# Handing the issue order of three engines to the scheduler, up to the last round of a Fourier transform and mixture-of-experts kernel

## Chip, core and metric

One core of one Trainium2 chip. The metric is the device time of one execution in microseconds (us); lower is better. TensorE (PE in the profile; PEld is its weight load), VectorE (DVE), ScalarE (ACT), GpSimd (POOL) and SyncE (SP, which only starts transfers here) each run their own instructions in the order in which the program lists them for that engine, and wait for one another through semaphores.

## The reference

The input `x` is 8 batches of 2496 tokens of 256 numbers. First a two-dimensional Fourier transform of each batch, of which the real part is kept; then every token goes to one of 8 experts:

```python
X = fft(fft(x, axis=1), axis=2).real          # per batch
x = X.reshape(19968, 256)
e_idx = argmax(x @ w_gate, axis=1)
gate_w = softmax(x @ w_gate)[e_idx]; eom = sigmoid(x @ w_output_gate)
for e in range(8):                             # F = 1024
    h = relu(x[e_idx == e] @ w1[e]); ye = h @ w2[e]
    out[e_idx == e] = gate_w * eom[:, e] * ye
```

## The kernel before, in words

There are two bodies of work. The **background** makes tokens, the **foreground** uses them.

*Background*, per batch b of 8, in five chunks: `xt` comes in by SP (512 KB each); `fold1` and `fold2` (L387 to L430) fold it by symmetry, on VectorE for batches under PF = 3, with `fold1` on GpSimd for the others; `square` (L383) or the activation in `fold2` sums its energy for a scale; `dstage` (L451) is the transform along the features, fp32 matmuls into PSUM; `devac` (L467) splits the result into two fp16 halves `ahi` and `alo` (ScalarE writes the first, VectorE the second); `sstage` (L513) is the transform along the sequence, fp16 matmuls; `sevac` (L528) combines its results into `rows`; `gating` (L564) chooses the expert and the destination row in some 30 small VectorE instructions with a matmul pair (L603, L604) among them; `scatter` (L667) writes 128 rows at a time to the DRAM buffer `scr`, sorted by expert, on GpSimd's queue. After certain batches `table_a` (L748) fixes which 256-row blocks are full; `table_b` (L766) does so for what is left.

*Foreground*: `experts` (L1363) goes through slots of up to 256 rows of one expert. The slots are grouped into rounds (ROUNDS, L40): three slots after batch 0, 13 after batch 1, 16 after batch 3, 16 after batch 5, and then the last round of 27 pairs and some smaller blocks after batch 7. For a slot, `load_x_` (L1213) brings the rows by a transposing transfer `xr` on SP; `load_w` (L1229) brings fp32 weights into `raw`; `conv` (L1258) splits them into two fp16 halves, ScalarE first (L1264) and VectorE after it (L1265), 1024 columns at a time, into a single weight buffer `wbuf`; `wenergy` (L1243) sums their squares on ScalarE. `mm1` (L1272) does 12 matmuls into the PSUM tile `hp` for each of four groups g of a slot; ScalarE (L1288, `hh`) and then VectorE (L1289, `hl`) take it out. `mm2` (L1291) does 12 matmuls into `yp`; after the fourth group ScalarE (L1311, `y`) takes it out and GpSimd's queue sends it to `out` (L1312). `hp` has two PSUM buffers and `yp` has one until the last round, `psb_t` (background) has two, `psm_t` one.

*Order.* The text writes an order by hand. In `experts` the `mm2` of a group comes LAG = 3 groups behind its `mm1`; `conv` calls stand between the groups. `start` (L926) writes the first batch, much of the second and the first weights line by line, and mixes three threads by weights (L1059). `background` (L1432) is a generator; the main loop (L1507 to L1523) takes a piece of it after each foreground step, paced by WORK (L66) and by cost figures that the pieces yield. `gating` and the folds yield pauses (GAP, L63), in which the other pieces go ahead.

`tc.manual_schedule()` makes every engine issue its instructions in the order of the text. With a set of engines, only those keep the order of the text; for the others the compiler's scheduler picks, each time an engine is free in its own simulated run of the program, among the instructions whose inputs it takes as ready, the one that stands first in the text. The order that it finds is fixed in the program; nothing is reordered on the chip. The data dependencies and the buffers are the same either way. Before the change one such region, with every engine, holds all of it:

```python
    with tc.manual_schedule():
        fg = experts()
        start(lambda: next(fg))
        rp.close()
        ...
        for m in fg:          # slots, with background() between them, until table_b is done
            ...
        for m in fg:          # the rest of the slots
            pass
```

Of the kernel before, what the change touches and what calls it, by code (L numbers as in the profile page):

```python
# [63 lines left out]
LB = 5  # L64
PF = 3
WORK = ((28.0, 13), (94.0, 112), (86.0, 140), (62.0, 117))  # L66
CONV = [mybir.EngineType.Activation, mybir.EngineType.DVE]
BIG = float(1 << 20)

# [158 lines left out]
def fft_moe_kernel(ctx: ExitStack, tc: tile.TileContext, xl, wg, w1, w2, tde, tdo, gt, ts0, tsm, tsr, tsq, cst, tid, out):  # L228
# [48 lines left out]
    if True:  # L277
# [17 lines left out]
        def load_x(n=NB * KC):  # L295

            while n and len(xq) < NB * KC:
                q = pw if held[pw] < NX2 and len(xq) < 2 * KC else px
                if held[q] == (NX2 if q is pw else NX):
                    break  # L300
                held[q] += 1
                b, c = divmod(len(xq), KC)
                t = q.tile([128, 8, HN], F32, name="xt", tag="xt", bufs=NX2 if q is pw else NX)
                nc.sync.dma_start(t, xl[b, c])
                xts[b, c] = t
                xq.append(q)
                n -= 1
# [205 lines left out]
        def sstage(b, i):  # L513
            s = st[b]
            if i == 0 and not routed(b):
                s["rows"] = []
                s["qs"] = pg.tile([128, 10, 32], F32, name="qs", tag="qs")
            ps = s["sps", i] = pool["b"].tile([128, 2, 512], F32, name="psb_t", tag="b")
            for k in range(2):
                for trig in range(2):  # L520
                    w = 129 if routed(b) else 145
                    src = 161 if routed(b) and trig else 145 * trig
                    for lhs, rhs, kw in s_terms(s, i, k, trig):
                        nc.tensor.matmul(ps[:, k, w * trig:w * trig + w], lhs, rhs[:, src:src + w], **kw)  # L524
                if k == 0:
                    yield "s"
# [617 lines left out]
    if True:  # L1144
# [8 lines left out]
        def add_wbuf(p_):  # L1153
            i = len(wbuf)
            wbuf.append([[p_.tile([128, 2, 1024], F16, name=f"w{m}b{i}{h}", bufs=1) for h in range(2)] for m in range(2)])
# [93 lines left out]
        def changed(n):  # L1249

            if n not in fresh:
                t, w, qi = table(n)
                need(sched[n][0])
                fresh.clear()
                fresh[n] = nc.values_load(t[0:1, 2 * w + qi:2 * w + qi + 1], engines=CONV, min_val=0, max_val=1)
            return fresh[n]
# [175 lines left out]
    def background():  # L1432
        def rest():
            yield from evac(1, 0)
            yield from c_s(1, 2)
            for _ in table_a(1):
                yield 0.13, 0
            scq.append(lambda: ready.add(1))

        yield from mix((g_(1), 2.0), (rest(), 12.0), (f_(2), 5.0))  # L1440
        yield from mix((c_d(2), 1.0))
        for b in range(2, NB):
            ths = [(c_s(b), 16.0)]
            if b + 1 < NB:
                ths.append((f_(b + 1), 11.0))
            yield from mix(*ths)
            for k, a in enumerate(BAS):
                if b == a and k not in begun:
                    scq.append(lambda k=k: k in begun or early(k, nc.sync.dma_start(fence, scr[DUM:DUM + 1, 0:1])))
            ths = [(g_(b), 9.5)]  # L1450
            if b + 1 < NB:
                ths.append((c_d(b + 1), 5.0))
            yield from mix(*ths)
            if b + 1 in BAS:
                k = BAS.index(b + 1)
                for _ in table_a(k):
                    yield 0.13
                scq.append(lambda k=k: ready.add(k))
        while scq:
            scq.pop(0)()  # L1460
        xp.close()
        for fill in (lambda: None, pads):
            fill()
            while deferred:
                deferred.pop(0)()
                yield 0.4
        for _ in table_b():
            yield 0.15
        pps.close()
        lp.close()  # L1470
        fx.append(pl(ctx, name="fr2", bufs=2))
        psf["h"] = pl(ctx, name="fpe2", bufs=1, space=PS)
        psf.update(hb=3, yb=2)
        add_raw(fx[1])
        add_wbuf(fx[1])
        ready.add(LAST)
# [7 lines left out]

    add_raw(fr0)
    add_wbuf(fr0)
    with tc.manual_schedule():
        fg = experts()
        start(lambda: next(fg))
        rp.close()  # L1490
        fx.append(pl(ctx, name="fr", bufs=2, side="right"))
        pps.close()
        pps = ExitStack()
        psf["h"] = pl(ctx, name="fpe", bufs=1, space=PS)
        psf.update(hb=2, yb=1)
        pool["b"] = pl(pps, name="psb2", bufs=2, space=PS)
        pool["m"] = pl(pps, name="psm2", bufs=1, space=PS)
        sums["t"] = pool["m"].tile([128, 512], F32, name="psm_t", tag="m")

        for i in range(2):  # L1500
            for _ in sstage(1, i):
                pass
        next(fg)
        load_x()
        bg = background()
        seg, acc, slot = 0, 0.0, 0
        for m in fg:  # L1507
            tick[0] += 1
            if m[0] == "slot":
                slot = m[1] + 1  # L1510
            while slot >= FIRST[seg + 1] - 1 and seg + 1 < LAST:
                seg += 1
            if scq and (tick[0] % 2 or not seg):
                scq.pop(0)()
            work, quanta = WORK[seg]
            acc = min(acc + work / quanta, 2.5)
            while acc > 0:
                c = next(bg, None)
                if c is None:
                    break  # L1520
                acc -= c
            if LAST in ready:
                break  # L1523
        for m in fg:
            pass

# [27 lines left out]
```

## Time and profile before

| | us |
|---|---|
| median of 2 runs | 1258.42 (1257.29 to 1259.56) |
| profiled execution, its own time | 1257.77 |
| its span, first to last instruction | 1256.0 |
| PE busy in the span | 1096.6 (87%) |
| DVE, ACT, POOL busy | 691.6, 608.5, 411.6 |
| mean granted TensorE clock | 0.941 of full |

The span is what the profile shows; 1.8 us lie around it. A busy share is an average over stages that differ, so the stages are looked at one by one. [...] In a table of waits the row `A <- B: 18.6, 10, 4.8` says that instructions of A waited for B 18.6 us in total, 10 times, 4.8 us at most; "issue" is idle time for which the profile shows no releaser, and a few per cent of matmul records can be missing, which also looks like that.

### The profile page before, as it was taken

To read this page: it belongs to the slowest core of one execution; us is meant where nothing else is said; L and a number is where in the kernel's file an instruction comes from. 1 tells how busy PE (TensorE), PEld (TensorE's weight loads), DVE (VectorE), ACT (ScalarE), POOL (GpSimd) and SP (SyncE) were. 2 spreads that over 40 slices of the span, in tenths; PEclk is the share of its full clock that TensorE was granted. 3 is DMA by queue.
4 is the path that set the end of the run, shared out by engine and by line. 5 is a ranking of instruction groups with operands and counts; after the bars stand their busy time and mean duration, and the time that the engine had idled before them with its cause. 6 is when DMAs were issued, how large, how long until landed. Compare 5 with 4: busy or idle time off the path is not lost. (4 is left out here: it accounts for less than half of the span.)

```text
span 1256.0 us, 27879 instructions
## 1 busy us (share of the span) xinstructions
PE 1096.6 (87%) x10226; PEld 953.0 (76%) x10226; DVE 691.6 (55%) x1373; ACT 608.5 (48%) x1107; POOL 411.6 (33%) x389
## 2 busy tenths in 40 slices
PE   6786589968898598999799887799999999999997
PEld 4665478757787487789588775588889999998997
DVE  5637466655665566666464363385435555545353
ACT  5635357535544544655453353345435545545453
POOL 0330531132336418527432255612211212122121
PEclk9867899989999799999899998899999999999999
DMA  9736426225642634844554164655447657546551
GB/s 355 279 113 167 139 77 193 76 85 139 166 108 95 213 83 129 229 116 107 147 134 110 59 167 137 164 125 156 110 129 170 156 151 183 150 113 173 148 130 33
DMA packets 154614, 179.44 MB, mean 143 GB/s; under 512 B 115563, under 2 KB 116461, under 8 KB 154466
## 3 DMA queue, kind: packets, MB, share of 16 engines
q1 hardware_dynamic: 138594, 134.87, 41.4%
q0 software_dynamic: 15728, 42.14, 9.9%
q8 instruction: 82, 1.34, 0.4%
q10 hardware_dynamic: 144, 0.55, 0.2%
q14 instruction: 66, 0.54, 0.2%
HBM read 157.92 MB, written 43.63 MB: 160 GB/s over the span
## 5 line engine op out<-in xcount | busy, mean ns | idle before, releaser
L1284 PE MATMUL hp<-xr,w0b 128*128 128x256 f16 (+2 forms) x4080 | 493.9, 271 | 37.4 <-issue 19.9
L1304 PE MATMUL yp<-w1b,hh 128*128 128x256 f16 x2560 | 453.0, 278 | 34.5 <-ACT y L1311 18.6
L1284 PEld LDWEIGHTS <-w0b 128*128 128x128 f16 x4080 | 386.3, 100 | 95.9 <-issue 46.2
L1312 POOL DMA_INDIRECT out_dram<-y,xf x160 | 173.7, 1085 | 703.7 <-ACT y L1311 669.8
L1289 DVE SCALAR_TENSOR_TENSOR hl<-hp,hh 128x512 f16<-128x512 f32 (+2 forms) x340 | 222.4, 655 | 318.7 <-ACT hh L1288 251.4
L1304 PE MATMUL yp<-w1b,hl 128*128 128x256 f16 x1280 | 355.5, 278 | 7.0 <-issue 6.6
L1288 ACT ACTIVATE hh<-hp 128x512 f16<-128x512 f32 (+2 forms) x340 | 192.0, 567 | 339.1 <-PE hp L1284 264.4
L1304 PEld LDWEIGHTS <-hh 128*128 128x128 f16 x2560 | 252.6, 100 | 77.3 <-issue 44.8
L668 POOL DMA_INDIRECT scr<-rows,desti x160 | 171.2, 1070 | 129.2 <-ACT qb L548 53.6
L1304 PEld LDWEIGHTS <-hl 128*128 128x128 f16 x1280 | 127.6, 100 | 24.5 <-issue 7.4
L1265 DVE SCALAR_TENSOR_TENSOR w1b<-raw1b,wsc,w1b 128x1024 f16<-128x1024 f32 x48 | 70.6, 1470 | 57.4 <-ACT w1b L1264 42.2
L1311 ACT ACTIVATE y<-yp,ysc 128x256 f32<-128x256 f32 (+1 forms) x160 | 67.3, 469 | 54.3 <-PE yp L1304 36.1
L460 PE MATMUL psb_t<-tdet,ft 128*125 128x290 f32 (+1 forms) x200 | 65.0, 476 | 18.1 <-DVE alo L473 4.0
L1265 DVE SCALAR_TENSOR_TENSOR w0b<-raw0b,wsc,w0b 128x1024 f16<-128x1024 f32 x48 | 61.9, 1292 | 23.1 <-ACT w0b L1264 16.5
L460 PEld LDWEIGHTS psb_t<-tdet,ft 128*125 128x125 f32 (+1 forms) x200 | 42.0, 220 | 35.7 <-issue 11.8
L1264 ACT ACTIVATE w1b<-raw1b,wsc 128x1024 f16<-128x1024 f32 x48 | 55.0, 1145 | 14.4 <-PE yp L1304 6.1
L1264 ACT ACTIVATE w0b<-raw0b,wsc 128x1024 f16<-128x1024 f32 x48 | 54.8, 1143 | 1.7 <-DVE wsc L272 1.7
L1265 DVE SCALAR_TENSOR_TENSOR w1b<-raw1b,ssc,w1b 128x1024 f16<-128x1024 f32 x32 | 41.0, 1282 | 23.4 <-ACT w1b L1264 14.6
L1265 DVE SCALAR_TENSOR_TENSOR w0b<-raw0b,ssc,w0b 128x1024 f16<-128x1024 f32 x32 | 40.8, 1282 | 19.5 <-ACT w0b L1264 17.4
L524 PE MATMUL psb_t<-ahi,tstq 125*128 125x145 f16 (+3 forms) x384 | 41.0, 230 | 7.1 <-DVE eo L550 4.6
L550 DVE SCALAR_TENSOR_TENSOR eo<-psb_t,qb 128x290 f32<-128x290 f32 (+1 forms) x64 | 25.8, 444 | 37.0 <-ACT qb L548 34.6
L524 PEld LDWEIGHTS <-tstq 125*128 125x128 f16 (+1 forms) x576 | 38.6, 100 | 9.5 <-DVE eo L550 4.8
(221 smaller groups left out, 1004.9 us busy)
## 6 DMA issues: line engine op xcount, KB each, us to landing
raw0b<-in_w_dram SPq DMA_DIRECT2D x126, 512.0 KB
raw1b<-in_w_dram SPq DMA_DIRECT2D x126, 512.0 KB
xt<-in_xl_dram SPq DMA_DIRECT2D x40, 512.0 KB
scr<-rows,desti POOLq DMA_INDIRECT x160
out_dram<-y,xf POOLq DMA_INDIRECT x160
xr<-scr SPq DMA_TRANSPOSE x85
xf<-scr SPq DMA_DIRECT2D x75, 2.0 KB
tst<-in_ts_dram SPq DMA_DIRECT2D x2, 512.0 KB
```

The source lines that it names most:

```text
L460: nc.tensor.matmul(o[:, 0:290], ft[:, k, par, W], tdab[:, k], start=(k == 0), stop=(k == 1))
L524: nc.tensor.matmul(ps[:, k, w * trig:w * trig + w], lhs, rhs[:, src:src + w], **kw)
L550: nc.vector.scalar_tensor_tensor(eo[:, k, W], ps[:HN, 0, W], 2.0 ** -SH, qb[:, W], op0=ALU.mult, op1=op)
L668: free_order("scr", batch=b, inst=nc.gpsimd.indirect_dma_start(out=scr[:, :], out_offset=bass.IndirectOffsetOnAxis(ap=s["desti"][:, j:j + ...
L1264: nc.scalar.activation(w[:, 0], r, AF.Copy, scale=sc)
L1265: nc.vector.scalar_tensor_tensor(w[:, 1], r, sc, w[:, 0], op0=ALU.mult, op1=ALU.subtract)
L1284: nc.tensor.matmul(ps[:, k, T], w1v[:, hl, kc, (f % 4) * 128:(f % 4 + 1) * 128], a["x"][:, x, T], start=(m == 0), stop=(m == 5))
L1288: nc.scalar.activation(hh[:, G, T], ps[:, :, T], AF.Relu)
L1289: nc.vector.scalar_tensor_tensor(hl[:, G, T], ps[:, :, T], 0.0, hh[:, G, T], op0=ALU.max, op1=ALU.subtract)
L1304: nc.tensor.matmul(a["yp"][0:M, u], a[k, h][:, f, u * 128:u * 128 + M], w2v[:, hl, f], start=(g == 0 and f == 0 and m == 0), stop=(h == 1 ...
L1311: nc.scalar.activation(a["y"][0:M, u], a["yp"][0:M, u], AF.Copy, scale=ys[0:M, u:u + 1])
L1312: put = nc.gpsimd.indirect_dma_start(out=out[:, :], out_offset=bass.IndirectOffsetOnAxis(ap=a["f"].bitcast(I32)[0:M, u, 1:2], axis=0), in_ ...
```

## The change

The one region becomes three. In the first (the first batch and what goes with it) and in the second (slots with background between them) only SP and GpSimd keep the order of the text; TensorE, ScalarE and VectorE are ordered by the scheduler. The third, the slots that are left when `table_b` is done, keeps the order of the text on all engines. No instruction is added or removed in the text, and no loop, buffer or pacing figure changes; the round of three slots after batch 0 stays.

```diff
@@ -64,6 +64,7 @@
 WORK = ((28.0, 13), (94.0, 112), (86.0, 140), (62.0, 117))
+PH1 = {mybir.EngineType.SP, mybir.EngineType.Pool}
 CONV = [mybir.EngineType.Activation, mybir.EngineType.DVE]
@@ -1484,9 +1485,10 @@
     add_raw(fr0)
     add_wbuf(fr0)
-    with tc.manual_schedule():
+    with tc.manual_schedule(engines=PH1):
         fg = experts()
         start(lambda: next(fg))
+    with tc.manual_schedule(engines=PH1):
         rp.close()
         fx.append(pl(ctx, name="fr", bufs=2, side="right"))
         pps.close()
@@ -1521,6 +1523,7 @@
                 acc -= c
             if LAST in ready:
                 break
+    with tc.manual_schedule():
         for m in fg:
             pass
```

## Rows read from the trace of the kernel before

**Rows 1.** Table of stretches, four stages of the span.

```profile
core 0: us, PE busy (x) PEld busy (x) DVE busy (x) ACT busy (x) POOL busy (x), PEclk, DMA share, GB/s
0.00:80.00 80.00, 54.71 (x476) 44.16 (x477) 46.38 (x138) 44.04 (x89) 17.17 (x22) 0.84 0.74 269
80.00:160.00 80.00, 51.39 (x556) 41.55 (x557) 45.11 (x108) 30.68 (x58) 22.50 (x22) 0.76 0.48 145
160.00:840.00 680.00, 588.71 (x5280) 505.38 (x5279) 397.20 (x837) 331.55 (x638) 283.61 (x266) 0.94 0.48 130
840.00:1240.00 400.00, 392.48 (x3801) 353.45 (x3800) 200.85 (x286) 199.33 (x318) 84.11 (x76) 1.00 0.57 144
```

**Rows 2.** Instructions that touch `ssc`, the last tile of `table_b`.

```profile
L735 DVE TENSOR_REDUCE ssc<-r_p x3: 485/486/486, 834.9 to 837.0; 128x40 f32<-128x320 f32 x3
```

**Rows 3.** Waits of PE, 0 to 160 us.

```profile
PE hp L1284 <- DVE hl L1289: 6.8, 4, 2.3
...
PE psb_t L524 <- DVE eo L550: 6.1, 2, 4.6
...
PE psm_t L603 <- DVE r_inc L599: 4.0, 1, 4.0
PE psb_t L460 <- ACT sq L385: 3.7, 1, 3.7
```

**Rows 4.** Waits of PE, 160 to 840 us.

```profile
PE yp L1304 <- issue: 22.1, 28, 4.3
PE yp L1304 <- ACT y L1311: 18.6, 10, 4.8
...
PE psm_t L438 <- DVE es L434: 7.5, 2, 6.9
PE psm_t L364 <- ACT r_ez L616: 6.9, 1, 6.9
PE psb_t L462 <- DVE alo L473: 5.0, 4, 2.5
PE psb_t L460 <- DVE alo L473: 4.0, 4, 1.4
...
PE hp L1284 <- DVE hl L1289: 1.2, 2, 0.6
```

**Rows 5.** Waits of PE, 840 us to the end.

```profile
PE hp L1284 <- DMA xr<-scr: 5.7, 2, 3.1
PE hp L1284 <- DVE hl L1289: 1.8, 2, 1.6
```

**Rows 6.** Groups by line, 0 to 840 us: evictions, weight conversions, folds.

```profile
L1289 DVE SCALAR_TENSOR_TENSOR hl<-hp,hh 128x512 f16<-128x512 f32 x168 | 115.3, 688 | 166.4 <-ACT hh L1288 142.9 <-issue 23.5
L1288 ACT ACTIVATE hh<-hp 128x512 f16<-128x512 f32 x168 | 99.2, 592 | 179.5 <-PE hp L1284 117.5 <-remote 45.6 <-PE yp L1304 6.4
...
L1265 DVE SCALAR_TENSOR_TENSOR w1b<-raw1b,wsc,w1b 128x1024 f16<-128x1024 f32 x42 | 62.9, 1497 | 49.0 <-ACT w1b L1264 35.7 <-issue 13.1
L1265 DVE SCALAR_TENSOR_TENSOR w0b<-raw0b,wsc,w0b 128x1024 f16<-128x1024 f32 x43 | 55.5, 1293 | 21.9 <-ACT w0b L1264 15.4 <-issue 4.8 <-DMA raw1b<-in_w_dram 1.5
...
L391 DVE TENSOR_TENSOR xt<-xt 128x500 f32<-128x500 f32 (+1 forms) x15 | 10.1, 676 | 3.2 <-ACT sq L385 3.2
```

**Rows 7.** Groups by line, 0 to 160 us: squares of the first weights.

```profile
L1245 ACT ACTIVATE wsq<-raw0b 128x1024 bf16<-128x1024 f32 x6 | 6.3, 1053 | 0.1
...
L1245 ACT ACTIVATE wsq<-raw1b 128x1024 bf16<-128x1024 f32 x6 | 6.3, 1047 | 0.0
```

**Rows 8.** Chain that ended last: start us, us, one group of 12 matmuls.

```profile
1156.00 1.31 PE yp L1304 x12
```

**Rows 9.** Timeline about 250 us, instructions in order of time.

```profile
249.29 7.21 DVE L1265 SCALAR_TENSOR_TENSOR w1b<-raw1b,wsc,w1b 128x1024 f16<-128x1024 f32 x1 [3.30 <-ACT w1b L1264]
249.34 6.07 POOL L391 TENSOR_TENSOR xt<-xt 128x500 f32<-128x500 f32 x5
...
258.43 0.56 PE L364 MATMUL psm_t<-wen,cs 128*128 128x1 f32 x2 [6.88 <-ACT r_ez L616]
```

## The prediction, blind

> **What bounds the kernel now.** I read the table of stretches first, to see which part of the run the change can reach at all [rows 1]. `table_b` ends at 837 us [rows 2], and from there on the slots keep the order of the text in both versions. In that part PE is busy 392.48 of 400 us at a granted clock of 1.00, so it is bound by matmuls, and its named waits come to 7.5 us [rows 1, 5]. What the scheduler is to order is the first 840 us. There PE is busy 54.71 and 51.39 of the first two 80 us, at clocks of 0.84 and 0.76, and 588.71 of the next 680 [rows 1]. So PE is idle for 53.9 us before 160 us and for 91.3 us after; no other engine is fuller (DVE 46.38 and 45.11 of 80 us in the first two stretches). The first 160 us are bound by chains that go from engine to engine, the rest mostly by PE, with holes.
>
> Second, the waits of PE say what the holes are. From 160 to 840 us the reader is to see four things: `yp` waits for ScalarE's eviction `y` (18.6 us, 10 times: there is one `yp` buffer), the small matmuls of the scales wait for `es` and `r_ez` (7.5 and 6.9 us), `psb_t` waits for `alo` (5.0 and 4.0 us), and 22.1 us of "issue" in 28 pieces with no releaser, part of which may be missing records [rows 4]. Before 160 us, `hp`, the transforms and the gating wait for VectorE and ScalarE, 6.8, 6.1, 4.0 and 3.7 us [rows 3]. All of these but "issue" are waits at the head of PE's list: PE stands still for one instruction while others further down may be ready. These are what another order could remove.
>
> **The change part by part.** *SP and GpSimd* keep the order of the text, so every transfer stays in its place among the transfers, at no cost in itself. They also tie the two bodies together: the output of a slot and the scatters of a batch share GpSimd's list, so neither body can run far ahead of the other.
>
> *TensorE, ScalarE, VectorE*: no instruction is added. What changes is which ready instruction goes first. There is a gain and a loss.
>
> Gain (D). When the head of PE's list is late, its list can now hold something else there. The named waits add up to 18.6 + (7.5 + 6.9 + 5.0 + 4.0) + (6.1 + 4.0 + 3.7) = 55.8 us, with those of `hp` for `hl` (6.8 and 1.2) 63.8 us [rows 3, 4]; that is the upper bound, and nothing the lower one. What can fill them is limited: one group is 1.31 us of PE [rows 8], and a group needs a free `hp` buffer of two, or the one `yp`. I take half of the 18.6 (9.3), since an `mm1` group is often free there; a third of the 23.4 (7.8); and a quarter of the 13.8 before 160 us (3.5), where the chain itself is the bound: 20.6 us.
>
> Loss (A), long work ahead of short work. The text puts each 1024-column conversion of weights at a chosen place between two evictions. A scheduler that takes what is ready starts a conversion as soon as the raw weights and the buffer allow it and VectorE or ScalarE has nothing earlier. The eviction that becomes ready just after it must then wait for the end. There are 42 + 43 such conversions on VectorE before 840 us, of 1.50 and 1.29 us, against 0.688 and 0.592 us for the two halves of an eviction [rows 6]. An eviction alone is 0.592 + 0.688 = 1.28 us, about the 1.31 us of the group that PE does into the other `hp` buffer [rows 6, 8]; with a conversion ahead of it, it is 2.6 to 2.8 us, and PE is 1.3 to 1.5 us short unless an `mm2` is ready. No row shows the wait in its new place; the nearest are the waits of `hp` for `hl` that are there now, 6.8 us in 4 and 1.2 us in 2, so 8.0 / 6 = 1.33 us each [rows 3, 4]. None of the 85 hurting gives 0, below which this term can't go (an early conversion frees no PE time by itself, and what it lets PE start sooner is counted in D); all of them hurting gives 85 x 1.33 = 113 us. I take three in ten, 25.5 x 1.33 = 34 us: many conversions are held until the last `mm1` has read the single weight buffer, as they are now.
>
> Loss (B), the first batch. In `start` the squares of the first weights and the folds of batch 1 stand behind steps of batch 0's chain. They are ready when their transfers land, so they can now go ahead of it: 6 + 6 squares of 1.05 us on ScalarE [rows 7] and 15 folds of 0.676 us on VectorE [rows 6]. All of them ahead of a chain step by their whole length is 12.6 + 10.1 = 22.7 us; none is 0, and a chain step that is pulled forward could give back at most the named 13.8 us of [rows 3], already in D. An instruction that is in the way is on average half done, so I take half: 11.4 us.
>
> [...]
>
> *Sum.* 34 + 11.4 - 20.6 = 24.8 us, x 1.4 = 34.7 us. The profiled execution took 1257.8 us (span 1256.0 and 1.8 around it), 0.6 us under the median of the runs shown; with the sum that is 1292.5, and I say 1292 us. The ends of the unknowns are far apart: all of D and none of A and B is -63.8 x 1.4 = -89 us (1169 us), all of A and B and no D is 135.7 x 1.4 = 190 us (1448 us).
>
> [...] At 249.29 us a conversion on VectorE takes 7.21 us in place of 1.29 (the mean of the `w0b` kind, in which no such case shows), while GpSimd does five folds of batch 3 in 6.07 us from 249.34, and PE then idles 6.88 us [rows 6, 9]. [...]
>
> **The rivals.**
> 1. *The holes are filled.* PE's waits are nearly all at the head of a list, which speaks for it; against it speaks that two `hp` buffers and one `yp` leave little to fill them with. Two thirds of D, 42.5 us, against one conversion in ten, 8.5 x 1.33 = 11.3 us, and no B: -31.2 x 1.4 = -44 us, 1214 us.
> 2. *The order hardly changes*, so the change doesn't do what it says. Between 160 and 840 us PE has something ready 87% of the time, ties go to the text, and SP's and GpSimd's lists stay. Gains and losses of 10 to 20 us cancel: 1258 us.
> [...]
> 4. *The first chain and the conversions go badly together*, the forecast's mechanism at a larger size: it decides where half of the conversions are picked as soon as they are ready. 42.5 x 1.33 + 22.7 - 10 = 69.2, x 1.4 = 97 us: 1355 us. For it speaks that ScalarE and VectorE are idle over 40% of the first 160 us, so that they often take whatever is ready.
>
> **How the numbers follow.** The forecast gets 0.37, and by itself would lie between 1268 and 1325 us. Rival 1 gets 0.15, rival 2 0.22, rival 3 0.05, rival 4 0.21. I think the losses likelier than the gains because D is bounded by 64 us of named waits, while every one of some hundred long instructions can end up ahead of a short one. A measurement of this kernel tells about 2% from no change, here 25 us. Rival 1 is faster by more than that (0.15); rivals 2 and 3 and the low end of the forecast, 0.05, are within it (0.32); the rest is slower (0.53). The range of 1222 to 1362 us leaves out most of rival 1 and the upper third of rival 4, some 0.2 together.
>
> **What would show it.** Right: before 840 us, PE's waits of `hp` for `hl` and of `yp` for `hl` grow from a few us to 30 or more, with a conversion or a square just ahead of the late eviction; the waits of `yp` for `y` shrink; `table_b` ends near 870 us; the stretch from there on is as long as before and full; the granted clock before 840 us is lower. Wrong: `table_b` ends before 820 us, or the waits of `hp` don't grow, or the time is lost after `table_b` or in waits for transfers.

## The result, and the profile after

The change made the kernel faster: 1187.78 us (1186.29 to 1189.27, 2 runs) against 1258.42, a ratio of 0.944 (95% interval 0.938 to 0.950). The forecast was slower by 34 us; the time lies below the low end of the range. The profiled execution took 1189.27 us, with a span of 1187.5: 68.5 us less than before.

The table of stretches of the kernel after, cut at 770 us, behind which about as many matmuls of slots are left (3882) as behind 840 us in the kernel before (3917); after an x stand the instructions that begin in a stretch, and PEclk is the granted clock as a share of full:

```profile
core 0: us, PE busy (x) PEld busy (x) DVE busy (x) ACT busy (x) POOL busy (x), PEclk, DMA share, GB/s
0.00:80.00 80.00, 52.15 (x570) 44.01 (x570) 57.18 (x182) 50.90 (x105) 17.50 (x22) 0.87 0.77 279
80.00:160.00 80.00, 66.51 (x657) 55.20 (x658) 45.33 (x109) 38.04 (x73) 36.92 (x34) 0.83 0.55 167
160.00:770.00 610.00, 555.46 (x5119) 483.13 (x5118) 378.06 (x795) 317.03 (x609) 281.31 (x256) 0.96 0.53 142
770.00:1170.00 400.00, 390.95 (x3758) 350.77 (x3756) 197.82 (x282) 196.30 (x313) 80.77 (x73) 0.99 0.56 141
```

Against [rows 1]: the first 80 us are no fuller on PE although DVE and ACT do more in them; from 80 to 160 us PE is 15 us fuller at a higher clock (0.83 against 0.76); the long stretch is 91% full against 87%, at a clock of 0.96 against 0.94; the last 400 us are as before. The instructions on `ssc` in the kernel after, against [rows 2]:

```profile
L736 DVE TENSOR_REDUCE ssc<-r_p x3: 474/476/477, 688.4 to 691.0; 128x40 f32<-128x320 f32 x3
```

`table_b` is done 146 us sooner, twice the gain. That milestone overstates it: the last matmul of the background ends only 84 us sooner (661 us against 745), and the rest is the table's own steps, which now end 25 us behind the last gating step and not 85; 4402 matmuls of slots are left behind `table_b` in place of 3929. The last scatter to `scr`, in GpSimd's list, leaves 69 us sooner. The scatters to `out`, counted in order, show the lead itself, here the first and the 45th, before and then after:

```profile
125.46 1.19 POOL L1312 DMA_INDIRECT out_dram<-y,xf  x1 [39.88 <-ACT y L1311]
561.05 0.97 POOL L1312 DMA_INDIRECT out_dram<-y,xf  x1 [13.37 <-ACT y L1311]
```

```profile
114.90 0.97 POOL L1313 DMA_INDIRECT out_dram<-y,xf  x1 [29.11 <-ACT y L1312]
491.40 0.97 POOL L1313 DMA_INDIRECT out_dram<-y,xf  x1 [10.40 <-ACT y L1312]
```

The lead is 11 us at the first slot, 27 at the second (178 us before), 36 at 269 us, 54 at 368, 64 at 440 and about 70 from 560 us on. So 27 of some 70 us are won by the second slot, the rest between it and 560 us, and nothing at the end.

The waits of PE in the kernel after, 0 to 160 us:

```profile
PE psm_t L506 <- issue: 12.3, 16, 2.5
PE psm_t L336 <- DMA wgt<-in_wg_dram: 6.5, 1, 6.5
PE psm_t L506 <- ACT car L650: 3.9, 1, 3.9
PE psb_t L461 <- ACT sq L386: 3.6, 1, 3.6
...
```

160 to 775 us:

```profile
PE hp L1285 <- DVE hl L1290: 17.5, 13, 5.2
PE hp L1285 <- issue: 15.9, 23, 1.6
PE yp L1305 <- issue: 10.0, 14, 1.0
PE yp L1305 <- ACT y L1312: 6.4, 2, 4.5
...
PE psm_t L604 <- DVE r_inc L600: 0.6, 1, 0.6
```

775 us to the end:

```profile
PE hp L1285 <- DMA xr<-scr: 5.2, 2, 3.2
PE hp L1285 <- DVE hl L1290: 3.7, 2, 2.5
```

Of the waits of [rows 3], those for `eo` and of `hp` for `hl` are gone, `r_inc` is down to 0.6 us and `sq` stays. Of [rows 4], the waits on `es`, `r_ez` and `alo` are gone, and `y` is down to a third; `hp` for `hl` has grown from 1.2 us in 2 to 17.5 us in 13. [Rows 5] stay, but for 1.9 us more of `hl`.

Where the time went, in five sums over all rows of PE's waits (short matmuls are those into `psb_t` and `psm_t` that wait for an engine), with PE's idle time as span less busy time:

| | span | PE busy | clock | PE idle | short | hp for hl | yp for y | hp for xr | issue |
|---|---|---|---|---|---|---|---|---|---|
| before | 1256.0 | 1096.6 | 0.941 | 159.4 | 53.8 | 9.9 | 18.6 | 5.7 | 55.3 |
| after | 1187.5 | 1075.4 | 0.953 | 112.1 | 15.2 | 21.2 | 6.4 | 5.2 | 48.7 |

The short matmuls give back 38.6 us and `y` 12.2; `hl` takes 11.3; "issue" and small rows make up the rest of 47.3 us less idle time. PE's busy time falls by 21.2 us with the same 10226 matmuls. Most of that is the clock. Within the two traces the granted clock is either 1.00 or 0.50 (0.50 from 74.3 to 91.2 us before, for one), and PE is busy for 110.0 us at 0.50 before and for 76.6 us after. In the trace of before, from the start of 12 matmuls of a slot to the start of the next ones it is 1.31 us at 1.00 (from 503.90 us) and 2.51 us at 0.50 (from 259.90). By that ratio, 33.4 us less at 0.50 make an estimated 16.0 us of the 21.2. Idle and busy together are 68.5 us.

What the 11.3 us are, in the timeline of the kernel after, around the longest such wait, on ScalarE and VectorE:

```profile
330.70 1.48 DVE L421 TENSOR_TENSOR ft<-xt 128x250 f32<-128x250 f32 x1
...
332.28 0.62 ACT L430 ACTIVATE sq<-ft 128x500 bf16<-128x500 f32 x1 [0.20 <-DVE ft L421]
...
332.90 1.13 ACT L1265 ACTIVATE w0b<-raw0b,wsc 128x1024 f16<-128x1024 f32 x1
...
333.94 0.57 ACT L1289 ACTIVATE hh<-hp 128x512 f16<-128x512 f32 x1
334.50 0.40 DVE L407 TENSOR_TENSOR ft<-xt 128x250 f32<-128x250 f32 x1
334.82 1.27 DVE L1266 SCALAR_TENSOR_TENSOR w0b<-raw0b,wsc,w0b 128x1024 f16<-128x1024 f32 x1
336.02 0.41 DVE L410 TENSOR_TENSOR xt<-xt 128x250 f32<-128x250 f32 x1
336.35 0.68 DVE L1290 SCALAR_TENSOR_TENSOR hl<-hp,hh 128x512 f16<-128x512 f32 x1
```

and on PE:

```profile
331.69 0.23 PE L525 MATMUL psb_t<-ahi,tstq 128*128 128x145 f16 x1
337.08 1.68 PE L1285 MATMUL hp<-xr,w0b 128*128 128x256 f16 x7 [5.17 <-DVE hl L1290]
```

PE has nothing for 5.17 us. ScalarE's half of the eviction (`hh` at 333.94) stands behind squares of the background and a conversion of 1.13 us, and VectorE's half, which needs it, then behind a fold, a conversion of 1.27 us and another fold. This is the loss that was forecast, but conversions are only a part of it: of all waits of `hp` for `hl` in this trace, 21.2 us, the conversions ahead of the late evictions on the two engines cover 5.3 us, the folds 5.0, other work of the background some 2, and most of the rest is the two halves of the eviction themselves.

### The profile page after: what moved, and what is told of

The parts are those of the page before. It is cut to its first block, busy times and chain, and to the rows that moved or that the text cites. A ratio compares the mean times of both kernels' runs of the same rounds, so it can differ in the third digit from the quotient of the medians.

```text
span 1187.5 us, 27938 instructions
## 1 busy us (share of the span) xinstructions
PE 1075.4 (91%) x10226; PEld 942.5 (79%) x10226; DVE 680.5 (57%) x1373; ACT 605.7 (51%) x1107; POOL 421.3 (35%) x389
## 5 line engine op out<-in xcount | busy, mean ns | idle before, releaser
L1285 PE MATMUL hp<-xr,w0b 128*128 128x256 f16 (+2 forms) x4080 | 492.7, 270 | 46.5 <-DVE hl L1290 21.2
L1305 PE MATMUL yp<-w1b,hh 128*128 128x256 f16 x2560 | 449.4, 277 | 13.3 <-issue 6.9
L1313 POOL DMA_INDIRECT out_dram<-y,xf x160 | 184.7, 1155 | 652.1 <-ACT y L1312 618.9
L669 POOL DMA_INDIRECT scr<-rows,desti x160 | 168.0, 1050 | 105.2 <-DMA raw1b<-in_w_dram 57.3
L1266 DVE SCALAR_TENSOR_TENSOR w0b<-raw0b,wsc,w0b 128x1024 f16<-128x1024 f32 x48 | 61.9, 1291 | 56.3 <-ACT w0b L1265 37.7
L1266 DVE SCALAR_TENSOR_TENSOR w1b<-raw1b,wsc,w1b 128x1024 f16<-128x1024 f32 x48 | 62.0, 1292 | 48.9 <-ACT w1b L1265 35.8
L461 PE MATMUL psb_t<-tdet,ft 128*125 128x290 f32 (+1 forms) x200 | 57.7, 428 | 7.1 <-ACT sq L386 3.6
L1265 ACT ACTIVATE w1b<-raw1b,wsc 128x1024 f16<-128x1024 f32 x48 | 54.9, 1146 | 17.1 <-remote 10.8
L461 PEld LDWEIGHTS psb_t<-tdet,ft 128*125 128x125 f32 (+1 forms) x200 | 37.1, 195 | 19.5 <-issue 6.3
L474 DVE SCALAR_TENSOR_TENSOR alo<-psb_t,p_x,ahi 125x580 f16<-125x580 f32 (+1 forms) x40 | 32.5, 818 | 26.0 <-ACT ahi L473 24.0
L525 PE MATMUL psb_t<-ahi,tstq 125*128 125x145 f16 (+3 forms) x384 | 43.4, 234 | 2.5 <-DVE rt L544 1.8
L473 ACT ACTIVATE ahi<-psb_t,p_x 125x580 f16<-125x580 f32 (+1 forms) x40 | 29.3, 740 | 30.6 <-PE hp L1285 12.5
```

The lines of the kernel that those rows point to most:

```text
L461: nc.tensor.matmul(o[:, 0:290], ft[:, k, par, W], tdab[:, k], start=(k == 0), stop=(k == 1))
L474: nc.vector.scalar_tensor_tensor(s["alo"][W, c], ps[W, :, 0:290], sc, s["ahi"][W, c], op0=ALU.mult, op1=ALU.subtract)
L669: free_order("scr", batch=b, inst=nc.gpsimd.indirect_dma_start(out=scr[:, :], out_offset=bass.IndirectOffsetOnAxis(ap=s["desti"][:, j:j + ...
L1265: nc.scalar.activation(w[:, 0], r, AF.Copy, scale=sc)
L1266: nc.vector.scalar_tensor_tensor(w[:, 1], r, sc, w[:, 0], op0=ALU.mult, op1=ALU.subtract)
L1285: nc.tensor.matmul(ps[:, k, T], w1v[:, hl, kc, (f % 4) * 128:(f % 4 + 1) * 128], a["x"][:, x, T], start=(m == 0), stop=(m == 5))
```

## The experiments

The runs were made in groups, each group on one chip and beside the kernel before. The chips differ: the kernel before takes 1255.66 us on the first and 1169.74, 1170.12, 1169.52 and 1172.18 us in the later groups. The chip of the pair above is not on record; its time is that of the first, and "the first chip" stands for both. The last section comes back to that. Ratios are to the kernel before on the same chip, intervals are 95%. Profiled spans and sums, each of one execution, are in the table behind the experiments. Edits are shown against the changed kernel, or against the kernel before where all engines keep the order of the text.

**Each region by itself** (before 1255.66 us). In the first run the scheduler orders only the first batch's region:

```diff
-    with tc.manual_schedule(engines=PH1):
+    with tc.manual_schedule():
         rp.close()
```

> Only the first region (the first batch) is left to the scheduler; the slots with background keep the order of the text. Two theories of where the 71 us come from. Theory P: PE's list skips the instruction that blocks its head, everywhere. Theory C: chains of one batch (gating, evictions, scatters) come earlier on ScalarE and VectorE, above all batch 1's, whose steps stand in the second region. The trace of the changed kernel has batch 0's gating 10 us later and the first output slot 29 us earlier. P expects a part here in proportion to the waits of PE in the first 85 us, some 5 to 15 us (1243 to 1253). C expects nothing or a loss, 1253 to 1268 us.

1252.38 us, 0.9995 (0.9961 to 1.003): nothing. The matmul of batch 0's gating starts at 45.8 us in place of 40.5, but the first slot's output leaves at 125 us in both. (In the changed kernel that output leaves 11 us sooner, not 29 as the expectation says.) This run is divided into the same three regions as the change, so that the division alone doesn't explain the gain either. In the second run only the region of the slots:

```diff
-    with tc.manual_schedule(engines=PH1):
+    with tc.manual_schedule():
         fg = experts()
```

> Only the second region (slots with background) is left to the scheduler; the first batch keeps the order of the text. Both theories expect most of the gain, P 55 to 65 of the 71 us (1193 to 1203), C all of it or a little more, since batch 0's chain is then not delayed: 1178 to 1190 us.

1193.34 us, 0.947 (0.943 to 0.952): within the intervals all of the gain. The short waits fall to 17.8 us.

**Which engine's list** (before 1255.66 us). TensorE alone freed:

```diff
-PH1 = {mybir.EngineType.SP, mybir.EngineType.Pool}
+PH1 = {mybir.EngineType.SP, mybir.EngineType.Pool, mybir.EngineType.Activation, mybir.EngineType.DVE}
```

> Only TensorE is left to the scheduler up to the last round; ScalarE and VectorE keep the order of the text with SP and GpSimd. P expects most of the gain: 1190 to 1210 us. C expects little, since evictions stay where they were and PE can only fill two buffers ahead: 1235 to 1255 us.

1235.54 us, 0.985 (0.980 to 0.989). Then ScalarE and VectorE freed, with TensorE in the order of the text:

```diff
-PH1 = {mybir.EngineType.SP, mybir.EngineType.Pool}
+PH1 = {mybir.EngineType.SP, mybir.EngineType.Pool, mybir.EngineType.PE}
```

> Only ScalarE and VectorE are left to the scheduler; TensorE keeps the order of the text. P expects little, as PE still stands at the head of its list: 1240 to 1260 us. C expects most of the gain: 1190 to 1215 us. If neither this nor the run with TensorE alone free gains much, the orders have to move together.

1213.59 us, 0.966 (0.962 to 0.970). The first rows of PE's waits in this run:

```profile
PE hp L1285 <- DVE hl L1290: 39.2, 17, 5.7
PE yp L1305 <- ACT y L1312: 16.6, 9, 7.7
```

This pair decides most. With PE's list fixed, the short waits fall all the same, from 53.8 to 13.6 us: they go because ScalarE and VectorE do the background's steps sooner, and PE need not step aside for that. The price is also there, 39.2 us of `hp` for `hl` in place of 9.9; of these, by the reading above, conversions ahead cover some 13 us. PE alone brings the short waits only to 34.5. With all three free, `hl` is back at 21.2 and `y` at 6.4. That PE's own list then covers the evictions that the other two have made late fits this, but isn't shown: the scheduler also gives the other two engines other lists when PE is free (516 of VectorE's 1373 instructions stand at another place in the two runs).

**One of the two evicting engines** (a later chip, before 1169.74 us), the set PH1 with PE and DVE added, then with PE and ACT added:

```diff
-PH1 = {mybir.EngineType.SP, mybir.EngineType.Pool}
+PH1 = {mybir.EngineType.SP, mybir.EngineType.Pool, mybir.EngineType.PE, mybir.EngineType.DVE}
```

> Only ScalarE is left to the scheduler up to the last round. Freeing TensorE alone gave 20 us, ScalarE and VectorE together 42 us. If each list holds up the work by itself, this and the run with VectorE alone add up to about 42 us, with some 15 to 25 us each (1230 to 1243). If the two only pay together, because a half of an eviction or conversion on one is followed by a half on the other, each gives under 10 us (over 1246).

1166.03 us, 0.996 (0.994 to 0.999).

```diff
-PH1 = {mybir.EngineType.SP, mybir.EngineType.Pool}
+PH1 = {mybir.EngineType.SP, mybir.EngineType.Pool, mybir.EngineType.PE, mybir.EngineType.Activation}
```

> Only VectorE is left to the scheduler up to the last round. Each list by itself: 15 to 25 us (1230 to 1243), and a little more than ScalarE alone, since VectorE has the gating chains, folds and the instructions that GpSimd's folds hold up. Only together: under 10 us (over 1246).

1149.04 us, 0.982 (0.977 to 0.987). VectorE's list alone gives 20.7 us, ScalarE's next to nothing. But the short waits, 59.2 us before, stay at 51.7 with ScalarE's list free and at 45.6 with VectorE's, where both together brought them to 13.6 on the first chip: these waits seem to need both lists, though both together were not run on this chip. VectorE's list by itself also takes 9.3 us off `y` (10.7 to 1.4).

**Before and after the table of batch 1** (same chip as the last two). The scheduler up to that table and the text behind it, then the other way round:

```diff
...
+        if 1 in ready and not switched:
+            switched = True
+            part.__exit__(None, None, None)
+            part = tc.manual_schedule(engines=ALL)
+            part.__enter__()
...
```

> All three engines are left to the scheduler up to the point of the text where the table after batch 1 is made; from there on the text's order holds. Counted by matmul work done, the changed kernel is some 26 us ahead by the first slots after that point and 69 us later on. Theory S (gains add up stage by stage): this gives 20 to 40 us, 1216 to 1236. Rival B (the early lead is only borrowed: foreground done sooner, background later): under 12 us, over 1244.

1160.52 us, 0.992 (0.990 to 0.995).

> The text's order holds up to the point where the table after batch 1 is made; from there on until the last round the scheduler orders the three engines. Theory S: what the other split leaves, 30 to 45 us, 1211 to 1226, and the two gains add up to 60 to 75 us. Rival B: 55 us or more, under 1202.

1160.54 us, 0.992 (0.989 to 0.995). Against the kernel before on a like chip, the scatters to `out` of the first lead by 16 us at the second slot and by 10.5 from 340 us on, and that stays to the end in the order of the text. Its short waits fall by 15.6 us, and the wait of the slots for their rows (`xr`) grows by as much, 8.4 to 24.1. The second leads by 11 us at 340 us, 16 at 419 and 9 to 15 behind that; it has 32.0 us of `hp` for `hl`. So each half is worth about 9 us and keeps the better part of its lead; the two add up to 18 of the 28.5 us that the whole change wins on a later chip. Why the whole is worth more than its halves wasn't tried.

**The change itself on a later chip** (before 1170.12 us).

> The changed kernel once more, beside the kernel before on the same chip. Theory (the lists skip waits at their heads, whatever the chip): the ratio of the named waits recovered, 42 us of idle by 1.4, is the same on every chip, so the ratio is near 0.945 here too. Rival (what the free order gains depends on the unnamed idle time of the slow chip): where the kernel before takes about 1255 us the ratio is 0.945; where it takes about 1170 us the gains of the two halves, 0.992 and 0.992, add to about 0.984 (1151 us).

1141.57 us, 0.976 (0.974 to 0.979): neither number, but nearer to the rival's. The gain is real but less than half as large, 28.5 us. Beside it the kernel before, unedited, for its profile there:

> The kernel before as a kernel of its own, for its profile on the same chip as the other three. If TensorE's unnamed idle time (55.3 us in the profile shown) belongs to the chip, it is under 5 us where the time is near 1170 us and over 35 us where it is near 1255 us; the named waits are 90 to 100 us in either. If it belongs to the kernel, it is 55 us on both.

1170.82 us, with 2.1 us of "issue" in place of 55.3: that idle time belongs to the chip. The named waits are 101.0 us (96.3 before on the first chip). First rows of PE's waits, kernel before on this chip:

```profile
PE hp L1284 <- DVE hl L1289: 13.0, 8, 3.6
PE yp L1304 <- ACT y L1311: 10.7, 6, 4.3
PE psm_t L438 <- DVE es L434: 10.2, 3, 6.9
PE hp L1284 <- DMA xr<-scr: 8.4, 4, 3.8
```

kernel after on this chip:

```profile
PE hp L1285 <- DMA xr<-scr: 24.4, 6, 6.7
PE hp L1285 <- DVE hl L1290: 21.3, 13, 5.2
PE psm_t L336 <- DMA wgt<-in_wg_dram: 6.5, 1, 6.5
PE yp L1305 <- ACT y L1312: 6.3, 2, 4.5
```

The short waits fall by as much as on the first chip (59.2 to 15.6), and `hl` grows by somewhat less (8.3). What differs: the slots now wait 16 us more for their rows, there was less to win at `y`, and the mean clock is 0.967 in both profiled executions, so that between these an idle microsecond less is worth 25.3 / 20.8 = 1.2 us of span in place of 68.5 / 47.3 = 1.4. Over all executions here the clock does rise a little, from 0.957 to 0.968 before to 0.967 to 0.972 after.

**Spacing and pace** (before 1170.12 us). The order of the text with the small matmuls six steps behind what they read:

```diff
-GAP = 3
+GAP = 6
```

> The order of the text on all engines, but with six steps instead of three between a short result and the small matmul that reads it. Theory (the gain is head-of-list waits at small matmuls): the waits on es, r_ez, r_inc and the columns' sums, some 24 us in the whole kernel before, go to under 10 us and the time falls by 15 to 25 us (ratio 0.98 to 0.988). Rival (what counts is the order among evictions and conversions, hidden by TensorE's own choice): these waits go, and the background's chains become longer by as much, so the time stays within 0.5 per cent.

1232.63 us, 1.055 (1.052 to 1.057): a miss. The background became late as a whole (`table_b` ends 106 us later than in the kernel before here), and the slots met it:

```profile
PE hp L1284 <- DMA xr<-scr: 56.6, 6, 28.9
PE hp L1284 <- DVE hl L1289: 37.7, 12, 12.8
```

The run mixes two things and says little of the short waits; it shows what a late background costs. The opposite, in the changed kernel:

```diff
-WORK = ((28.0, 13), (94.0, 112), (86.0, 140), (62.0, 117))
+WORK = ((28.0, 13), (94.0, 112), (86.0, 125), (62.0, 100))
```

> The changed kernel with the background spread over fewer steps in its two later segments (125 for 140 and 100 for 117). Theory (TensorE's idle time is already down to a few waits in this stretch): the last table ends some 40 to 50 us sooner and the time moves by less than 0.5 per cent against the changed kernel. Rival (the order is still thin of matmuls that are ready): a denser background gives up to 1 per cent more. Third: conversions and evictions crowd, the wait of the second matmul on hl grows above 30 us, and the time rises by 1 per cent.

1133.67 us, 0.970 (0.968 to 0.973), against 0.976 (0.974 to 0.979) for the change as it is, on the same chip. This is the lowest ratio of the study, though the intervals of the next best overlap with it. The same edit in the order of the text, and a still denser one (110 and 85) in the changed kernel, on another chip (before 1169.52 us):

> The order of the text with the denser background (125 for 140, 100 for 117). Theory (only an order that steps over waits can take a denser background): the waits at the heads of lists come closer together, the time is 0 to 1 per cent longer than before (ratio 1.000 to 1.010). Rival (the pace alone is worth 0.7 per cent in either order): ratio 0.993.

1179.92 us, 1.009 (1.006 to 1.012).

> The changed kernel with the background still denser (110 steps for 140 and 85 for 117). Theory (held by the arrival of gathered rows and by hl): the rows' wait falls a little further from 21 us, the hl wait rises from 15 us, and the time stays within 0.7 per cent of the run with 125 and 100. Rival (denser is better without end): another 8 us, ratio 0.7 per cent lower. Third: conversions crowd the evictions and the ratio is 1 per cent higher.

1138.48 us, 0.973 (0.968 to 0.978). So the pace alone gives nothing: in the text's order it loses, in the scheduler's it wins a little, and the next step shows no further gain; the wait for `xr` is then 28.6 us.

Then the spacing cut from three to one, in the changed kernel and in the kernel before:

```diff
-GAP = 3
+GAP = 1
```

> The changed kernel with one step instead of three between a short result and the small matmul that reads it. Theory (the scheduler steps over the wait, so the text's spacing is not needed): the waits of the small matmuls stay under 5 us together after 160 us, and the time is within 0.7 per cent of the changed kernel, rather shorter because the background's chains are. Rival (the scheduler keeps near the text and the spacing does the hiding): 15 to 25 us of such waits come back and the time rises by 1.5 to 2 per cent.

1144.1 us, 0.978 (0.973 to 0.982): as the changed kernel. The short waits are 16.0 us, all before 160 us.

> The order of the text with one step instead of three. Theory (waits at the heads of lists): the waits of the small matmuls (sums, energies, basem, eo, alo), some 43 us in the kernel before on this kind of chip, grow by 20 to 40 us and the time rises by 2 to 4 per cent (ratio 1.02 to 1.04). Rival (these waits are covered anyway): ratio within 0.7 per cent of 1. Third: the shorter chains give back as much as the waits take, which would show as grown waits with an equal time.

1185.47 us, 1.013 (1.009 to 1.016): slower, but not by the mechanism that was expected. The short waits are 60.5 us against 59.2. PE is idle 5.3 us more and busy 11.1 us more at a mean clock of 0.951 against 0.967 in the profiled executions; of that, the stretch where the clock differs most, first in the kernel before on a like chip, then here:

```profile
160.00:400.00 240.00, 209.01 (x1963) 184.51 (x1961) 158.91 (x333) 140.77 (x279) 91.62 (x87) 0.95 0.52 146
```

```profile
160.00:400.00 240.00, 207.68 (x1863) 181.07 (x1863) 152.03 (x317) 135.18 (x269) 85.19 (x82) 0.91 0.49 137
```

The pair shows that the free order doesn't need the text's spacing and that the text's order does. That the text loses through longer short waits, it refutes; why the clock is lower was not found.

**The two engines that the change leaves in the text** (before 1172.18 us), with the pace of 125 and 100. SP free too, then GpSimd free too and SP not:

```diff
-PH1 = {mybir.EngineType.SP, mybir.EngineType.Pool}
+PH1 = {mybir.EngineType.Pool}
```

> The changed kernel with the denser background (125 and 100) and SP's list left to the scheduler as well; GpSimd alone keeps the text. If the rows come late because gathers stand behind weight loads in SP's text, the rows' wait falls from 21 us to under 10 and the time by 1 per cent against the run with that pace (ratio 0.96). If they aren't computed sooner, the wait and the time stay (0.970). Third: the scheduler puts weight loads ahead of gathers, the wait doubles, and the ratio is 0.98 or more.

1137.78 us, 0.972 (0.969 to 0.976): the same as with SP in the text; the wait for `xr` is 25.3 us.

```diff
-PH1 = {mybir.EngineType.SP, mybir.EngineType.Pool}
+PH1 = {mybir.EngineType.SP}
```

> The same with GpSimd's list left to the scheduler and SP in the order of the text. If the scatters come late because GpSimd's list holds them behind output scatters and folds, the rows' wait falls from 21 us to under 10 and the time by 1 per cent (ratio 0.96). If the rows aren't computed sooner, both stay (0.970). Third: folds and output scatters are drawn ahead of scatters to scr, the wait grows, and the ratio is 0.98 or more.

1150.09 us, 0.982 (0.978 to 0.985), with these first rows of PE's waits:

```profile
PE hp L1285 <- DVE hl L1290: 31.5, 12, 9.3
PE hp L1285 <- DMA xr<-scr: 13.3, 3, 7.7
PE yp L1305 <- ACT y L1312: 11.1, 4, 6.5
```

So GpSimd's list does set when the rows come: with it free the 60th and the 120th scatter to `scr` start at 251 and 504 us, in the text at that pace at 302 and 545, and the wait for `xr` is 13.3 us in place of 21.3. But freeing it doubles the wait for `hl` (14.9 to 31.5) and adds 3.8 us at `y`. SP's list has no visible part in it. Leaving GpSimd in the text, as the change does, is the better choice of the two; for SP it makes no difference. The round after the last table was never tried under the scheduler.

The profiles of all runs, as in the table above (the first four belong beside 1256.0 and 1187.5, the others beside the two rows at their head, some of them from a like chip and not the same one):

| | span | PE busy | clock | short | hl | y | xr | issue |
|---|---|---|---|---|---|---|---|---|
| first batch free | 1249.3 | 1092.5 | 0.941 | 58.3 | 10.6 | 18.5 | 8.3 | 41.7 |
| slots free | 1195.4 | 1082.4 | 0.950 | 17.8 | 25.7 | 5.6 | 9.6 | 40.5 |
| PE free | 1233.5 | 1088.5 | 0.940 | 34.5 | 16.8 | 10.4 | 8.1 | 48.3 |
| ACT, DVE free | 1209.2 | 1079.5 | 0.947 | 13.6 | 39.2 | 16.6 | 6.3 | 36.0 |
| *before* | 1169.1 | 1059.3 | 0.967 | 59.2 | 13.0 | 10.7 | 8.4 | 2.1 |
| *after* | 1143.8 | 1054.8 | 0.967 | 15.6 | 21.3 | 6.3 | 24.4 | 2.8 |
| ACT free | 1161.6 | 1058.6 | 0.967 | 51.7 | 7.1 | 10.9 | 13.5 | 2.6 |
| DVE free | 1149.7 | 1056.2 | 0.967 | 45.6 | 20.5 | 1.4 | 8.6 | 1.9 |
| free until batch 1 | 1158.1 | 1055.1 | 0.963 | 43.6 | 5.7 | 10.7 | 24.1 | 2.7 |
| free after batch 1 | 1155.2 | 1057.9 | 0.966 | 29.1 | 32.0 | 6.2 | 13.1 | 1.8 |
| text, GAP 6 | 1231.1 | 1069.8 | 0.940 | 42.7 | 37.7 | 8.9 | 56.6 | 1.9 |
| text, pace | 1177.0 | 1065.2 | 0.960 | 57.2 | 11.0 | 15.4 | 7.9 | 3.0 |
| text, GAP 1 | 1185.5 | 1070.4 | 0.951 | 60.5 | 14.6 | 13.5 | 9.0 | 2.2 |
| after, pace | 1127.1 | 1045.0 | 0.976 | 15.9 | 14.9 | 7.3 | 21.3 | 3.3 |
| after, denser pace | 1138.2 | 1054.2 | 0.969 | 15.5 | 16.8 | 3.2 | 28.6 | 2.2 |
| after, GAP 1 | 1139.9 | 1052.3 | 0.971 | 16.0 | 12.4 | 10.9 | 26.4 | 2.5 |
| pace, SP free | 1133.8 | 1049.8 | 0.969 | 20.4 | 15.0 | 6.9 | 25.3 | 2.2 |
| pace, GpSimd free | 1147.9 | 1058.6 | 0.962 | 17.1 | 31.5 | 11.1 | 13.3 | 2.5 |

## Why the prediction was wrong

*What bounds it: right.* The stretch behind `table_b` is as full as before (390.95 of 400 us against 392.48), and what was won is the waits at the heads of PE's list before it, and PE's busy time beside them, at a mean clock of 0.953 in place of 0.941.

*D, the gain: mis-sized, and this is the step that failed first.* It was taken as 20.6 us of 55.8, a half, a third and a quarter of three parts. The rows of these three parts gave back 12.2 of 18.6, all of the 23.4 and 9.6 of 13.8 us, 45.2 in all; with the short waits that the forecast didn't name and those that are new, the two classes gave back 50.8 us (38.6 and 12.2). The fractions came from PE's side alone. With PE's list fixed, the short waits fell as far (to 13.6 us, against 15.2): the results that PE waited for were late because they stood in ScalarE's and VectorE's lists behind other instructions, and those lists were freed too. The named waits did bound the gain; the limit of `hp` and `yp` buffers didn't apply to the part that is won at the producer.

*A, late evictions: right mechanism, wrong place of the other half.* Forecast 34 us. With PE fixed, `hp` for `hl` grew by 29.3 us, close to it. With all three lists free it grew by 11.3, the very number of rival 1. Both agreements are in part luck, since the forecast counted conversions alone and folds stand ahead of the late evictions as well. The step that failed is "PE is 1.3 to 1.5 us short unless an `mm2` is ready", of which three in ten were to hurt: the waits grew by a third of that, probably because with PE's list free PE mostly has something ready. The loss was priced as if PE kept its old list, the gain as if only PE got a new one.

*B, the first batch: it happened and cost nothing.* Batch 0's gating matmul starts 10 us later in the changed kernel, close to the 11.4 us of the forecast; but the first slot's matmuls start only 2.5 us later (95.5 us against 93.0), its output leaves 11 us sooner, and with the first region alone under the scheduler, which delays that matmul by 5.3 us, the time doesn't move. How the delay is made good wasn't tried by itself. Its term was also misread: of the 15 folds in [rows 6] only five are of batch 1 (28.6 to 62.8 us); five are batch 0's own and five batch 2's.

*The sum.* D is off by 30.2 us, A by 22.7 and B by 11.4, together 64.3 us; by its 1.4 that is 90 of the 104 us between 1292 and 1188. *The factor of 1.4*, taken for what the clock adds to each us lost or won, is a term that no run shows. What the runs showed is that 68.5 us of span went with 47.3 us less of PE's idle time in the pair above, which is 1.4 too, and 25.3 with 20.8 between the two profiled executions on the later chip, 1.2.

*The 22.1 us of "issue"* were rightly left out of the gain (all of PE's "issue" moved by 6.6 us), but for a wrong reason: they are no missing records, since the same program shows 2.1 us elsewhere, with the same 10226 matmuls in its trace.

*The rivals.* Rival 1 named what happened, with 0.15; its D of 42.5 us was still 8 us short, which by 1.4 is 12 of the 26 us between its 1214 and 1188. *GpSimd's folds.* The two 6.9 us waits of [rows 4], of which one follows the conversion of 7.21 us in [rows 9], are gone with all the others, so that the time tells nothing of them by themselves. VectorE's instructions that run beside a GpSimd fold take 22.0 us longer in all than the median of their kind before and 28.6 us after, but the worst single one loses 5.9 us before and 1.6 after. The fold at 330.70 above, 1.48 us long in place of 0.41 while GpSimd does one of 1.45 us from 330.46, is of this kind. The nine evictions `hl` that run beside a fold before are not: they take 0.68 to 0.69 us, and the longest of the others 0.69. *The signs:* "`table_b` ends before 820 us" was named as a sign of being wrong, and it ended at 691. Of the signs of being right only the shrinking of `y` came; `hp` for `hl` reached 21 us and not 30, and the clock before the last part rose.

## What to carry to other kernels

When several lists are freed at once, price gain and loss with all of them free: a late result is brought forward by its producers' lists (here by two of them: the short waits, 59.2 us before, stayed at 51.7 and 45.6 with either alone and fell to 13.6 from 53.8 with both, on another chip), whatever the consumer's list can put into the hole. Waits at the head of a consumer's list, if the producers' lists are freed too, can come back for the most part (here 50.8 of 72.4 us in the two classes), at a price in other waits (11.3 us). Read the lead from the last body of work (outputs), not from a milestone of the other body, and measure on more than one chip: here one edit was worth 5.6% on one and 2.4% on another.

## What was not expected of the hardware

The same program took 1256.0 us (span) on one chip and 1169.1 on another. Of those 86.9 us, 53.2 are PE's "issue" idle time (55.3 in 77 pieces against 2.1 in 1), and PE is busy 37.3 us less, at a mean clock of 0.967 against 0.941; the named waits are about equal. VectorE shows the same, 58.9 us of "issue" against none. On the first chip most of these pieces, 64 of 77, lie within 0.5 us of one of GpSimd's scatters to `scr`, for example, on GpSimd in the timeline of the kernel before (first chip):

```profile
495.12 0.97 POOL L668 DMA_INDIRECT scr<-rows,desti  x1 [0.30 <-issue]
496.39 2.00 POOL L668 DMA_INDIRECT scr<-rows,desti  x1 [0.30 <-issue]
```

and on PE:

```profile
495.63 0.27 PE L1304 MATMUL yp<-w1b,hh 128*128 128x256 f16 x1 [0.66 <-issue]
495.74 0.27 PE L1304 MATMUL yp<-w1b,hl 128*128 128x256 f16 x1
497.11 0.38 PE L1304 MATMUL yp<-w1b,hh 128*128 128x256 f16 x2 [1.09 <-issue]
```

The instructions of one matmul group stop in the middle, and the profile shows nothing that they wait for. On the later chips the same bursts are there and such pieces are not: PE's "issue" is 1.8 to 3.3 us in all their profiles, and in the kernel before there, GpSimd starts five scatters to `scr` from 458.89 to 464.13 us while PE's groups of 12, by turns into `hp` and `yp`, begin every 1.31 us from 455.17 to 465.65. What makes the first chip stop was not found, and whether it is why the change gains more there was only argued, from the sums: with PE held up by the chip, the rows of a slot have time to come, and the wait for `xr` is 5.2 us in place of 24.4.
